# Window attention with two feed-forward stages on one core: the first four attention units multiply float32 as it is, and ScalarE issues four of the first loads

## The chip, the cores and the metric

One NeuronCore of a Trainium2 chip runs the whole program in one launch. The metric is the device time of one execution in microseconds (us). Engines are called as in the profile: PE (TensorE, with PEld for its weight loads), ACT (ScalarE), DVE (VectorE), POOL (GpSimd), SP (SyncE, which here only issues DMAs).

## What is computed

Three parts follow each other. q and k come as the reference draws them; only shapes matter here.

```python
# attention: B=2, H=8, S=576, D=64; window 128, causal, linear bias per head
scores = scale * q @ k.T ; masked to 0 <= i-j < 128, plus bias
attn   = softmax(scores) ; out = attn @ v             # float32
x      = out, heads joined: 1152 tokens x 512
# four experts, all of them for every token: h = relu(x @ w1[e]); y += p[:, e] * (h @ w2[e])
# last: h = relu(y @ w_in); out = (h * h) @ w_out      # w_in 512x2048, w_out 2048x512
```

Float32 accuracy is asked for. The kernel gets it by splitting each operand into a rounded part (float32r, "hi") and the rest ("lo") and adding up the products of the parts that matter.

## The kernel before, in words

**Attention** is cut into 20 units. The first four (numbers 0 to 3, one pair of heads each, `t0 == 0`) hold the first 128 queries of both batches: four score blocks of 128x128 each. The other sixteen hold two query tiles of one batch, with a window of two key tiles. For each unit the tasks are, in the names of the code: `load_q`, `load_k`, `load_v` (SP issues them, into the tiles `rq`, `rk`, `rv`); `qh`, `ql` (hi and lo of q), `kh`, `kl` (hi and lo of k, stacked in the 128 partitions of `khl`), `vh`, `vl` (hi and lo of v, written into two padded tiles); then per query tile `scores` (tile `sc`, two matmuls per head: `khl` with `qh`, `khl` with `ql`), `top` (DVE adds the bias and takes the extreme), `exp` (ACT), `inv` (DVE), `norm` (POOL), `turn` (PE transposes into `tp`), `hi` and `lo` (tile `pt`, both parts of the weights); and at the end `pv` (tile `xps`: per pair of heads and block three products, hi-hi, hi-lo, lo-hi, for each head), `evh`, `evl` (into `xh`, `xl`).

**The expert weights** are loaded as float32 (`wraw`) and split into `wh`, `wl` by ACT, DVE and POOL. The first expert's matmuls (`hps` for the first product, `yacc` for the second) run between the attention units as soon as their tokens are there.

**The order** of all this is set by a list planner (`Plan`): each task has prices per engine, dependencies, buffers that it takes (`SLOTS` gives the number of each) and a due time. At each step it takes the engine that can start first, and on it the task that is due first. A PE task that starts before `COLD` is priced 1.7 times as long. What it emits is a fixed order on each engine, in which every instruction waits for semaphores. Transfers use eight semaphores in turn (`DMAHW0` to `DMAHW7`), and a transfer is issued only when the one before it on the same semaphore has landed. After the planned part, from the second expert on, the order is a plain loop: four experts and two halves of the last stage, PE all the time.

The names that the change touches: `Plan.COLD`, `SLOTS["rv"]`, `VS` (blocks per `rv` tile), `unit_tasks` with `load_q`, `load_k`, `load_v` and `pv`, `job_tasks` with `scores` and `hi`, the due times at the calls, and `T0`.

Of the kernel before, what the change touches and what calls it, by code (L numbers as in the profile page):

```python
# [8 lines left out]
F32 = mybir.dt.float32  # L9
F32R = mybir.dt.float32r  # L10
# [6 lines left out]
P = 128  # L17
# [17 lines left out]
class Plan:  # L35
# [4 lines left out]

    LOOK = 0.15
    OTHER = 0.3
    COLD = 28.0

    def __init__(self, slots):
        self.tasks = []
# [80 lines left out]
def kernel(  # L127
# [14 lines left out]
    nc = tc.nc  # L142
    B, H, _, S = qT.shape
# [170 lines left out]
    def chunks(e):  # L314
# [1 line left out]


    SLOTS = dict(
        rq=3, rk=3, rv=2, qh=2, ql=2, khl=2, vp=2, sc=2, tp=2, ts=5, st=5, pt=2, work=2, y=2, h=4
    )  # L320
    plan = Plan(SLOTS)
    actx = ExitStack()
# [13 lines left out]
    def a_tile(kind, shape, dtype):  # L336
        return asp.tile(shape, dtype, tag=kind, name=kind, bufs=SLOTS[kind])
# [12 lines left out]
    def act(n, lat=0.1):  # L350
        return ("ACT", 0.1 + 0.00083 * n, 0.1 + 0.00083 * n + lat)

    def dve(n, lat=0.05):
        return ("DVE", 0.15 + 0.00105 * n, 0.15 + 0.00105 * n + lat)

    def gps(n, lat=0.05):
        return ("POOL", 0.2 + 0.0021 * n, 0.2 + 0.0021 * n + lat)

    def pe(us):
        return ("PE", us, us + 0.25)  # L360
# [28 lines left out]
                    out=bias[:, h, cs], in0=rel[:, cs], scalar1=scale, scalar2=None, op0=ALU.mult  # L389
                )  # L390

    VS = 4
    vpad = []
    for i in range(2):
        vh = abias.tile([P, VS, 3, D], F32R, name=f"vh{i}")
# [15 lines left out]
    def unit_tasks(u, due):  # L411
# [30 lines left out]

        def load_v(eng):
            t = b_["rv"].tile = a_tile("rv", [P, VS, 2 * D], F32)
            cs = slice(c * 2 * D, (c + 1) * 2 * D)
            for i, b in enumerate(bs):
                nc.sync.dma_start(
                    out=t[:, i * full:(i + 1) * full, :],
                    in_=v[b, k0:k0 + full * P, cs].rearrange("(k p) d -> p k d", p=P),
                )  # L450
                if left:
                    nc.sync.dma_start(out=t[0:left, full, :], in_=v[b, k0 + full * P:q1, cs])

        def dma(kb, n):
            return [("SP", max(0.5 * n, kb / 210.0), max(0.5 * n, kb / 210.0) + 2.2)]
# [31 lines left out]
        def vl(eng):  # L487
            for r, k in parts:
# [2 lines left out]
        end = due[-1]  # L491
        first = due[0]
        kbytes = nb * 2 * D * 4 / 1024.0
        lq = add("lq", dma(2 * kbytes * nq, nb), load_q, takes=[b_["rq"]], due=first - 12.0,
                 follow=[task.get(("lq", u - 1))])
        lk = add("lk", dma(kbytes * nk, nb), load_k, takes=[b_["rk"]], due=first - 11.9,
                 follow=[task.get(("lk", u - 1))])
        lv = add("lv", dma(kbytes * nk, nb + bool(left)), load_v, takes=[b_["rv"]],
                 due=end - 9.0, follow=[task.get(("lv", u - 1))])
        tqh = add("qh", [act(G * nq), dve(G * nq)], qh, shared=True, deps=[lq], takes=[b_["qh"]],  # L500
                  bufs=[b_["rq"]], due=first - 9.0)
        tkh = add("kh", [act(G * nk), dve(G * nk)], kh, shared=True, deps=[lk], takes=[b_["khl"]],
                  bufs=[b_["rk"]], due=first - 9.1)
        tql = add("ql", [gps(G * nq), dve(G * nq)], ql, shared=True, deps=[tqh], takes=[b_["ql"]],
                  bufs=[b_["rq"], b_["qh"]], due=first - 8.2)
        tkl = add("kl", [dve(G * nk), gps(G * nk)], kl, shared=True, deps=[tkh],
                  bufs=[b_["rk"], b_["khl"]], due=first - 8.3)
        nv = nb * nk
        tvh = add("vh", [act(nv), dve(nv)], vh, shared=True, deps=[lv, task["zero", u % 2]], takes=[b_["vp"]],
                  bufs=[b_["rv"]], due=end - 3.4)  # L510
        tvl = add("vl", [gps(nv), dve(nv)], vl, shared=True, deps=[tvh], bufs=[b_["rv"], b_["vp"]],
                  due=end - 2.6)

        split = []
        wide = 0
# [1 line left out]
            wide += tile_n(t) * (1 if t == 0 else 2)  # L517
        pos = 0
        for i, t in enumerate(range(t0, t1)):
            split += job_tasks(u, i, t, add, b_, due[i], [tqh, tql, tkh, tkl], G, q0, k0, pos, wide)  # L520
            pos += tile_n(t) * (1 if t == 0 else 2)

        mm = []
# [35 lines left out]
        def evl(eng):  # L559
            rest(eng, xl[:, c, cols], b_["work"].tile, xh[:, c, cols])  # L560

        tpv = add("pv", [pe(sum(3 * (max(0.107, w * 0.00046) + max(0.06, w * 0.00046))
                                for *_, w in mm))], pv,
                  deps=split + [tvh, tvl], takes=[b_["work"]], bufs=[b_["pt"], b_["vp"]],
                  due=end - 1.3, follow=[prev["pv"]])
        teh = add("evh", [act(nb * nq), dve(nb * nq)], evh, deps=[tpv], bufs=[b_["work"]],
                  due=end - 0.9)
# [2 lines left out]
    def job_tasks(u, i, t, add, b_, end, ready, G, q0, k0, pos, wide):  # L570
# [16 lines left out]
        def scores(eng):  # L587
            sc = s["sc"].tile = ps_tile("sc", [P, G, w], "sc")
            qs = slice(t * P - q0, t * P - q0 + n)
            for g in range(G):  # L590
                for ql in (b_["qh"].tile, b_["ql"].tile):
# [54 lines left out]
            parts = [(r, k * n, n) for k, r in enumerate(rows)]  # L646

        def hi(eng):
            if i == 0:
# [16 lines left out]

        tb = [task["bias", c, True]] + ([task["bias", c, False]] if t else [])
        tsc = stage("sc", [pe(2 * G * max(0.107, w * 0.00047))], scores, 7.4, deps=ready,
                    takes=[s["sc"]], bufs=[b_["qh"], b_["ql"], b_["khl"]])
# [9 lines left out]
        m = G * len(cols) * n  # L679
        thi = stage("hi", [act(m), dve(m)], hi, 2.0, deps=[ttp],  # L680
                    takes=[b_["pt"]] if i == 0 else [], bufs=[s["tp"]] + ([b_["pt"]] if i else []))
        tlo = stage("lo", [dve(m)], lo, 1.5, deps=[thi], bufs=[s["tp"], b_["pt"]])
        return [thi, tlo]

# [400 lines left out]
```

## Time and profile before

| | |
|---|---|
| median of 3 runs | 706.04 us (705.80 to 706.08) |
| profiled execution | 706.03 us; its span, first to last instruction, 704.2 us |
| busy share of the span | PE 98%, PEld 88%, DVE 45%, ACT 38%, POOL 30% |
| chain that ended last | PE 89% of the span, nearly all of it `yacc` and `hps` |
| DMA | 48.12 MB, mean 68 GB/s |
| granted TensorE clock | 1.00 in every slice of the page |

Busy PE time counts a matmul from its start to its end, and matmuls overlap; how fast PE goes is read from the distance between the starts of two that follow each other (called the pitch below). Engines other than PE cost time only where PE waits for them.

### The profile page before, as it was taken

The page shows a single profiled execution, that of the slowest core. Times are in us where ns is not written, and L with a number is a line of the kernel's source. Part 1 is how long each engine was busy: PE and PEld are TensorE (multiplying, and loading weights), DVE is VectorE, ACT ScalarE, POOL GpSimd, SP SyncE. Part 2 cuts the span into 40 slices and gives each one's busy share as a digit, 9 for nine tenths or more (in the row PEclk, how much of TensorE's full clock was granted, in tenths as well). Part 3 has the DMA queues.
Part 4 walks back from the last instruction along what each step waited for, and adds up shares of the span by engine and source line. Part 5 has one row for each costly group of instructions (what it writes and reads, how often), then busy time and mean ns, then how long its engine had stood idle before and what let it go on. Part 6 is the DMA issues. An engine that isn't in the chain of part 4 may idle for free.

```text
span 704.2 us, 9937 instructions
## 1 busy us (share of the span) xinstructions
PE 686.7 (98%) x3796; PEld 622.1 (88%) x3796; DVE 314.0 (45%) x718; ACT 264.4 (38%) x606; POOL 211.8 (30%) x222
## 2 busy tenths in 40 slices
PE   4999999999999999999999999999999999999997
PEld 3889898889999999999999999999999999999996
DVE  6789888732121212121122655527786627112121
ACT  6898576624331112311112322314354434322221
POOL 5899756407550003510011000000232222222221
PEclk9999999999999999999999999999999999999999
DMA  5863321223410001310005500035400120001011
GB/s 144 236 205 98 92 75 46 70 95 116 125 56 0 1 28 62 120 31 0 1 31 177 182 2 0 31 108 197 144 1 1 31 90 1 1 0 46 1 45 46
DMA packets 39137, 48.12 MB, mean 68 GB/s; under 512 B 3633, under 2 KB 27697, under 8 KB 39089
## 3 DMA queue, kind: packets, MB, share of 16 engines
q1 hardware_dynamic: 39088, 47.48, 21.6%
q8 instruction: 30, 0.49, 0.3%
q14 instruction: 19, 0.15, 0.1%
HBM read 45.11 MB, written 2.36 MB: 67 GB/s over the span
## 4 chain that ended last, share of the span: by engine, by line
PE 89%; DVE 0%; issue 0%
PE yacc L740 41%; PE hps L706 41%; PE xps L547 3%; PE tp L638 1%; PE sc L592 1%; PE xtp L772 1%; DVE y L764 0%
## 5 line engine op out<-in xcount | busy, mean ns | idle before, releaser
L706 PE MATMUL hps<-xh,wh 128*128 128x384 f32 (+1 forms) x608 | 201.9, 332 | 0.8 <-DVE xl L347 0.5
L706 PE MATMUL hps<-xl,wh 128*128 128x384 f32 (+1 forms) x608 | 199.8, 329 | 1.1 <-DVE xl L347 1.1
L706 PE MATMUL hps<-xh,wl 128*128 128x384 f32 (+1 forms) x608 | 200.2, 329 | 0.0
L740 PE MATMUL yacc<-wh,hl 128*128 128x512 f32 x432 | 170.9, 396 | 0.0
L740 PE MATMUL yacc<-wl,hh 128*128 128x512 f32 x432 | 170.6, 395 | 0.0
L740 PE MATMUL yacc<-wh,hh 128*128 128x512 f32 x432 | 168.9, 391 | 0.0
L722 DVE SCALAR_TENSOR_TENSOR hl<-hps,hh 128x384 fp32r<-128x384 f32 x80 | 44.6, 558 | 227.6 <-ACT hh L721 227.6
L721 ACT ACTIVATE hh<-hps 128x384 fp32r<-128x384 f32 x80 | 39.3, 491 | 245.1 <-PE hps L706 245.1
L730 POOL TENSOR_TENSOR hl<-r,hh 128x384 fp32r<-128x384 f32 x48 | 50.8, 1059 | 265.9 <-ACT hh L729 265.9
L706 PEld LDWEIGHTS hps<-xh,wh 128*128 128x128 f32 x608 | 114.9, 189 | 7.0 <-issue 0.7
L706 PEld LDWEIGHTS hps<-xl,wh 128*128 128x128 f32 x608 | 114.8, 189 | 6.6 <-DVE xl L347 1.4
L706 PEld LDWEIGHTS hps<-xh,wl 128*128 128x128 f32 x608 | 114.7, 189 | 0.0
L273 POOL TENSOR_TENSOR wl<-wraw,wh 128x1024 fp32r<-128x1024 f32 x24 | 57.2, 2390 | 175.3 <-ACT wh L271 167.9
L740 PEld LDWEIGHTS yacc<-wh,hl 128*128 128x128 f32 x432 | 81.1, 188 | 17.4
L740 PEld LDWEIGHTS yacc<-wl,hh 128*128 128x128 f32 x432 | 81.1, 188 | 13.2
L740 PEld LDWEIGHTS yacc<-wh,hh 128*128 128x128 f32 x432 | 81.3, 188 | 12.6
L728 DVE TENSOR_TENSOR r<-hps,r 128x384 f32<-128x384 f32 x48 | 26.7, 556 | 102.6 <-ACT r L727 102.6
L727 ACT ACTIVATE r<-hps 128x384 f32<-128x384 f32 x48 | 23.6, 491 | 92.0 <-PE hps L706 92.0
L628 POOL TENSOR_SCALAR ts<-ts,st 128x256 f32<-128x256 f32 (+2 forms) x80 | 40.0, 514 | 22.9 <-DVE st L623 18.1
L613 ACT ACTIVATE ts<-ts,st 128x256 f32<-128x256 f32 (+2 forms) x80 | 37.1, 466 | 5.0 <-DVE st L604 5.0
L729 ACT ACTIVATE hh<-r 128x384 fp32r<-128x384 f32 x48 | 25.2, 526 | 35.6 <-DVE r L728 35.6
L547 PE MATMUL xps<-pt,vh 128*128 128x128 f32 (+3 forms) x224 | 34.9, 261 | 0.0
(71 smaller groups left out, 715.3 us busy)
## 6 DMA issues: line engine op xcount, KB each, us to landing
wraw<-in_w_dram SPq DMA_DIRECT2D x32, 512.0 KB, 4.1
wraw<-in_w_in_dram SPq DMA_DIRECT2D x16, 512.0 KB, 4.1
wraw<-in_w_out_dram SPq DMA_DIRECT2D x16, 512.0 KB, 4.5
rq<-in_qT_dram SPq DMA_DIRECT2D x8, 256.0 KB, 4.2
out_dram<-y SPq DMA_DIRECT2D x8, 256.0 KB, 2.1
rk<-in_kT_dram SPq DMA_DIRECT2D x8, 192.0 KB, 5.0
rv<-in_v_dram SPq DMA_DIRECT2D x8, 192.0 KB, 2.6
rq<-in_qT_dram SPq DMA_DIRECT2D x8, 192.0 KB, 2.4
```

What stands on the lines that cost most here:

```text
L273: eng.tensor_tensor(out=lo[:, ks, :], in0=full, in1=f32(hi[:, ks, :]), op=ALU.subtract)
L547: nc.tensor.matmul(out=xps[0:rows, o0:o0 + w], lhsT=l_, rhs=r_, start=start, stop=(i == len(mm) - 1 and a == 0 and l_ is wl_), skip_group_ ...
L613: nc.scalar.activation(out=ts[0:n, g, :], in_=ts[0:n, g, :], func=ACTF.Exp, bias=st[0:n, 0, g:g + 1], scale=-1.0, accum_out=st[0:n, 1, g:g ...
L628: nc.gpsimd.tensor_scalar(out=ts[0:n, g, :], in0=ts[0:n, g, :], scalar1=st[0:n, 2, g:g + 1], scalar2=1.0, op0=ALU.mult, op1=ALU.mult,)
L706: nc.tensor.matmul(out=ps, lhsT=l_[:, k, cs], rhs=r_[:, k, cols], start=(k == 0 and r_ is xh and l_ is wh and not second), stop=(k == KT - ...
L721: nc.scalar.activation(out=hh, in_=ps, func=ACTF.Relu)
L722: nc.vector.scalar_tensor_tensor(out=hl, in0=ps, scalar=0.0, in1=f32(hh), op0=ALU.max, op1=ALU.subtract)
L727: nc.scalar.activation(out=r, in_=ps, func=ACTF.Relu)
L728: nc.vector.tensor_tensor(out=r, in0=ps, in1=r, op=ALU.mult)
L729: nc.scalar.activation(out=hh, in_=r, func=ACTF.Copy)
L730: nc.gpsimd.tensor_tensor(out=hl, in0=r, in1=f32(hh), op=ALU.subtract)
L740: nc.tensor.matmul(out=y, lhsT=l_[:, ns], rhs=r_[:, fo, :], start=(f == 0 and j == 0), stop=(f == FT - 1 and j == 2),)
```

## The change

The first four units (`raw`) no longer split q, k, v and the softmax weights: q is loaded once into 64 partitions, the score matmul takes `rk` and `rq` as float32, one per head; the transposed weights are copied to `pt` once; and `pv` takes `rv` and `pt` as float32, one matmul of 64 columns per head and batch. In units 0 and 1 the second batch's part of q and k is issued from ACT's queue. v of a raw unit is one transfer, `rv` tiles have three blocks and there are four of them. The planner gets other numbers: COLD, the due times of all units and of the first weights.

```diff
-    COLD = 28.0
+    COLD = 20.0
...
-        rq=3, rk=3, rv=2, qh=2, ...
+        rq=3, rk=3, rv=4, qh=2, ...
...
-    VS = 4
+    VS = 3
...
+        raw = t0 == 0
...
         def load_q(eng):
+            r = D if raw else P
             t = b_["rq"].tile = a_tile("rq", [P, G, nq], F32)
             for i, b in enumerate(bs):
-                nc.sync.dma_start(
-                    out=t[:, 2 * i:2 * i + 2, :],
-                    in_=qT[b, 2 * c:2 * c + 2, :, q0:q1].rearrange("a p s -> p a s"),
+                (nc.scalar if i and u < 2 else nc.sync).dma_start(
+                    out=t[0:r, 2 * i:2 * i + 2, :],
+                    in_=qT[b, 2 * c:2 * c + 2, 0:r, q0:q1].rearrange("a p s -> p a s"),
                 )
         def load_k(eng):
...
-                nc.sync.dma_start(
+                (nc.scalar if i and u < 2 else nc.sync).dma_start(
...
         def load_v(eng):
...
+            if raw:
                 nc.sync.dma_start(
+                    out=t[:, 0:nb, :], in_=v[:, 0:P, cs].rearrange("b p d -> p b d")
+                )
+                return
...
-        tqh = add("qh", ...)
+        if not raw:
+            tqh = add("qh", ...)
...
         def pv(eng):
             xps = b_["work"].tile = ps_tile("work", [P, nb * nq], "xps")
+            if raw:
+                for i in range(nb):
+                    for a in range(2):
+                        nc.tensor.matmul(
+                            out=xps[a * D:(a + 1) * D, i * P:(i + 1) * P],
+                            lhsT=b_["rv"].tile[:, i, a * D:(a + 1) * D],
+                            rhs=b_["pt"].tile[:, 2 * i + a, :], start=True, stop=True,
+                            skip_group_check=True,
+                        )
+                return
...
             for g in range(G):
+                if raw:
+                    nc.tensor.matmul(
+                        out=sc[0:n, g, :], lhsT=b_["rq"].tile[0:D, g, qs],
+                        rhs=b_["rk"].tile[:, g, j0:j0 + w], start=True, stop=True,
+                    )
+                    continue
...
+        if raw:
+            return [thi]
         tlo = stage("lo", [dve(m)], lo, 1.5, deps=[thi], bufs=[s["tp"], b_["pt"]])
...
-            unit_tasks(u, [20.0 + 2.0 * u])
+            unit_tasks(u, [14.0 + 2.0 * u])
...
-            end = 45.0 + 5.5 * (u - NP)
+            end = 38.0 + 5.5 * (u - NP)
...
-    T0, T1, ITEM = 34.0, 34.0, 4.2
+    T0, T1, ITEM = 24.0, 34.0, 4.2
```

Three places where the order moves. **ACT, from its first instruction**; `rq`, `rk` are the raw loads, `bias` the table of biases, `ts` the scores in softmax, and what an instruction waits for stands in brackets (DMAHW0 to 7 are the transfers' semaphores). Before:

```order
L384 ACT_TABLE_LOAD
L384 ACTIVATE bias<-rel 128x128 [waits Pool_49]
L384 ACTIVATE bias<-rel 128x128 x5
L341 ACTIVATE qh<-rq 128x512 [waits DMAHW1_49,DMAHW0_49]
L341 ACTIVATE khl<-rk 64x512 [waits DMAHW3_49,DMAHW2_49]
```

And now:

```order
L434 DMA rq<-in_qT_dram 64x2x128
L442 DMA rk<-in_kT_dram 64x2x128
L434 DMA rq<-in_qT_dram 64x2x128
L384 ACT_TABLE_LOAD
L384 ACTIVATE bias<-rel 128x128 [waits Pool_49]
L384 ACTIVATE bias<-rel 128x128
L442 DMA rk<-in_kT_dram 64x2x128 [waits DMAHW5_49]
L384 ACTIVATE bias<-rel 128x128 x4
L643 ACTIVATE ts,st<-ts,st 128x128 [waits DVE_49] x12
```

The splits of q and k are gone from the front, four transfers have come in, and the fourth of them, the second batch's k of unit 1, waits for the fifth of the transfers' semaphores, ahead of four biases and all exponentials.

**SP, from its first instruction**, as it is now:

```order
L434 DMA rq<-in_qT_dram 64x2x128
L442 DMA rk<-in_kT_dram 64x2x128
L434 DMA rq<-in_qT_dram 64x2x128
L442 DMA rk<-in_kT_dram 64x2x128
L451 DMA rv<-in_v_dram 128x2x128
L434 DMA rq<-in_qT_dram 64x2x128 [waits DMAHW0_49]
L434 DMA rq<-in_qT_dram 64x2x128 [waits DMAHW1_49]
L442 DMA rk<-in_kT_dram 64x2x128 [waits DMAHW2_49]
L442 DMA rk<-in_kT_dram 64x2x128 [waits DMAHW3_49]
L451 DMA rv<-in_v_dram 128x2x128 [waits DMAHW4_49]
L434 DMA rq<-in_qT_dram 64x2x128 [waits DMAHW5_49,PE_49]
```

Before, SP's first four rows were two q and two k transfers of unit 0 alone. The third and the eleventh row here are the first and second transfer on semaphore DMAHW5; the eleventh is unit 3's first q, which also waits for the scores of unit 0 on PE. ACT's fourth transfer waits for a count of 32 on that semaphore, which is both of them landed.

**PE, at the end of the last 128-wide scores.** Before, a piece of 48 matmuls for `xps` in the four units begins like this:

```order
L592 MATMUL sc<-khl,ql 128x128
L547 MATMUL xps<-pt,vh_97 128x128 x2
L547 MATMUL xps<-pt,vl_98 128x128
L547 MATMUL xps<-pt,vh_97 64x128 x2
L547 MATMUL xps<-pt,vl_98 64x128
```

And now PE's whole beginning is:

```order
L616 MATMUL sc<-rk,rq 128x128 x16
L668 MATMUL tp<-ident,ts 128x128 x8
L554 MATMUL xps<-pt,rv 64x128 x8
L668 MATMUL tp<-ident,ts 128x128 x8
L745 MATMUL hps<-xh,wh 128x256
L745 MATMUL hps<-xl,wh 128x256
L745 MATMUL hps<-xh,wl 128x256
L554 MATMUL xps<-pt,rv 64x128 x8
```

32 score matmuls of the four units have become 16, 48 for `xps` have become 16, and all four units' scores now stand ahead of the first transposes.

## Rows read from the trace of the kernel before

**Rows 1.** Busy time by stretch (stretch, length, engines (xinstructions), granted clock, DMA share, GB/s).

```profile
0.00:10.00 10.00, 3.21 (x14) 3.02 (x15) 5.79 (x22) 5.75 (x13) 4.05 (x14) 1.00 0.49 126
0.00:20.00 20.00, 10.09 (x42) 8.76 (x43) 12.69 (x55) 12.92 (x41) 11.76 (x26) 1.00 0.63 159
20.00:50.00 30.00, 27.89 (x201) 25.70 (x200) 24.95 (x69) 26.86 (x73) 27.57 (x33) 1.00 0.81 233
50.00:80.00 30.00, 28.35 (x219) 26.04 (x218) 26.68 (x74) 23.42 (x64) 28.28 (x32) 1.00 0.33 91
80.00:120.00 40.00, 40.00 (x324) 36.85 (x323) 34.13 (x111) 28.14 (x89) 23.78 (x40) 1.00 0.25 67
```

**Rows 2.** PE's waits, whole span: for whom, total us, times, longest.

```profile
PE sc L592 <- DVE khl L347: 6.8, 2, 6.4
PE sc L592 <- POOL khl L347: 3.1, 2, 2.3
```

**Rows 3.** Timeline, PE from 17.3 to 30.7 (start us, us, engine, line, operation).

```profile
17.32 0.47 PE L592 MATMUL sc<-khl,qh 128*128 128x128 f32 x1 [0.87 <-POOL khl L347]
17.59 0.41 PE L592 MATMUL sc<-khl,ql 128*128 128x128 f32 x1
17.80 0.42 PE L592 MATMUL sc<-khl,qh 128*128 128x128 f32 x1
...
25.49 1.08 PE L638 MATMUL tp<-ident,ts 128*128 128x128 f32 x4
...
26.79 0.41 PE L592 MATMUL sc<-khl,qh 128*128 128x256 f32 x1
27.00 0.41 PE L592 MATMUL sc<-khl,ql 128*128 128x256 f32 x1
...
28.44 0.28 PE L592 MATMUL sc<-khl,qh 128*128 128x256 f32 x1
28.55 0.28 PE L592 MATMUL sc<-khl,ql 128*128 128x256 f32 x1
...
30.68 0.33 PE L706 MATMUL hps<-xh,wh 128*128 128x256 f32 x1
```

**Rows 4.** Timeline, all engines, the first 8 us; SPq is SP issuing.

```profile
0.73 0.96 SPq L430 DMA_DIRECT2D rq<-in_qT_dram  x2
...
4.34 1.26 SPq L438 DMA_DIRECT2D rk<-in_kT_dram  x2
...
5.64 1.07 SPq L447 DMA_DIRECT2D rv<-in_v_dram  x2
...
6.44 0.48 PE L592 MATMUL sc<-khl,qh 128*128 128x128 f32 x1 [6.44 <-DVE khl L347]
...
7.36 0.63 ACT L341 ACTIVATE khl<-rk 64x512 fp32r<-64x512 f32 x1 [0.50 <-DMA rk<-in_kT_dram]
```

**Rows 5.** Groups by line and shape, ACT to 160 us: busy us, mean ns.

```profile
L341 ACT ACTIVATE qh<-rq 128x512 fp32r<-128x512 f32 x12 | 7.5, 626 | 4.4 <-DMA rq<-in_qT_dram 3.3 <-DVE st L604 1.1
...
L613 ACT ACTIVATE ts<-ts,st 128x128 f32<-128x128 f32 x16 | 6.2, 388 | 0.0
...
L341 ACT ACTIVATE vh<-rv 128x256 fp32r<-128x256 f32 x10 | 4.1, 410 | 0.5 <-DMA rv<-in_v_dram 0.5
...
L384 ACT ACTIVATE bias<-rel 128x128 bf16<-128x128 f32 x6 | 1.3, 296 | 0.1
L384 ACT ACT_TABLE_LOAD x1 | 1.3, 1283 | 0.7 <-PEq L1075 0.7
```

**Rows 6.** Timeline, POOL from 13 to 19.

```profile
13.01 0.73 POOL L347 TENSOR_TENSOR vl<-rv,vh 128x256 fp32r<-128x256 f32 x1
13.72 2.20 POOL L628 TENSOR_SCALAR ts<-ts,st 128x128 f32<-128x128 f32 x4
16.01 1.26 POOL L347 TENSOR_TENSOR khl<-rk,khl 64x512 fp32r<-64x512 f32 x1
17.36 1.41 POOL L628 TENSOR_SCALAR ts<-ts,st 128x128 f32<-128x128 f32 x4
```

More of the change, by code (lines that the diff above doesn't have):

```diff
@@ L318 @@
     SLOTS = dict(
-        rq=3, rk=3, rv=2, qh=2, ql=2, khl=2, vp=2, sc=2, tp=2, ts=5, st=5, pt=2, work=2, y=2, h=4
+        rq=3, rk=3, rv=4, qh=2, ql=2, khl=2, vp=2, sc=2, tp=2, ts=5, st=5, pt=2, work=2, y=2, h=4
     )
@@ L445, in load_v @@
             cs = slice(c * 2 * D, (c + 1) * 2 * D)
-            for i, b in enumerate(bs):
+            if raw:
                 nc.sync.dma_start(
-                    out=t[:, i * full:(i + 1) * full, :],
-                    in_=v[b, k0:k0 + full * P, cs].rearrange("(k p) d -> p k d", p=P),
-                )
-                if left:
-                    nc.sync.dma_start(out=t[0:left, full, :], in_=v[b, k0 + full * P:q1, cs])
+                    out=t[:, 0:nb, :], in_=v[:, 0:P, cs].rearrange("b p d -> p b d")
+                )
+                return
+            b = bs[0]
+            nc.sync.dma_start(
+                out=t[:, 0:full, :],
+                in_=v[b, k0:k0 + full * P, cs].rearrange("(k p) d -> p k d", p=P),
+            )
+            if left:
+                nc.sync.dma_start(out=t[0:left, full, :], in_=v[b, k0 + full * P:q1, cs])
         def dma(kb, n):
@@ L493, in unit_tasks @@
         kbytes = nb * 2 * D * 4 / 1024.0
-        lq = add("lq", dma(2 * kbytes * nq, nb), load_q, takes=[b_["rq"]], due=first - 12.0,
+        lq = add("lq", dma((1 if raw else 2) * kbytes * nq, 1 if u < 2 else nb), load_q, takes=[b_["rq"]], due=first - 12.0,
                  follow=[task.get(("lq", u - 1))])
-        lk = add("lk", dma(kbytes * nk, nb), load_k, takes=[b_["rk"]], due=first - 11.9,
+        lk = add("lk", dma(kbytes * nk, 1 if u < 2 else nb), load_k, takes=[b_["rk"]], due=first - 11.9,
@@ L497, in unit_tasks @@
                  follow=[task.get(("lk", u - 1))])
-        lv = add("lv", dma(kbytes * nk, nb + bool(left)), load_v, takes=[b_["rv"]],
+        lv = add("lv", dma(kbytes * nk, 1 + bool(left)), load_v, takes=[b_["rv"]],
                  due=end - 9.0, follow=[task.get(("lv", u - 1))])
[L500 to L512, printed above, removed]
+        if not raw:
+            tqh = add("qh", [act(G * nq), dve(G * nq)], qh, shared=True, deps=[lq], takes=[b_["qh"]],
+                      bufs=[b_["rq"]], due=first - 9.0)
+            tkh = add("kh", [act(G * nk), dve(G * nk)], kh, shared=True, deps=[lk], takes=[b_["khl"]],
+                      bufs=[b_["rk"]], due=first - 9.1)
+            tql = add("ql", [gps(G * nq), dve(G * nq)], ql, shared=True, deps=[tqh], takes=[b_["ql"]],
+                      bufs=[b_["rq"], b_["qh"]], due=first - 8.2)
+            tkl = add("kl", [dve(G * nk), gps(G * nk)], kl, shared=True, deps=[tkh],
+                      bufs=[b_["rk"], b_["khl"]], due=first - 8.3)
+            nv = nb * nk
+            tvh = add("vh", [act(nv), dve(nv)], vh, shared=True, deps=[lv, task["zero", u % 2]], takes=[b_["vp"]],
+                      bufs=[b_["rv"]], due=end - 3.4)
+            tvl = add("vl", [gps(nv), dve(nv)], vl, shared=True, deps=[tvh], bufs=[b_["rv"], b_["vp"]],
+                      due=end - 2.6)
@@ L519, in unit_tasks @@
         for i, t in enumerate(range(t0, t1)):
-            split += job_tasks(u, i, t, add, b_, due[i], [tqh, tql, tkh, tkl], G, q0, k0, pos, wide)
+            split += job_tasks(
+                u, i, t, add, b_, due[i], [lq, lk] if raw else [tqh, tql, tkh, tkl], G, q0, k0,
+                pos, wide,
+            )
             pos += tile_n(t) * (1 if t == 0 else 2)
@@ L560, in evl @@
             rest(eng, xl[:, c, cols], b_["work"].tile, xh[:, c, cols])
-        tpv = add("pv", [pe(sum(3 * (max(0.107, w * 0.00046) + max(0.06, w * 0.00046))
-                                for *_, w in mm))], pv,
-                  deps=split + [tvh, tvl], takes=[b_["work"]], bufs=[b_["pt"], b_["vp"]],
+        us = sum(3 * (max(0.107, w * 0.00046) + max(0.06, w * 0.00046)) for *_, w in mm)
+        tpv = add("pv", [pe(1.0 if raw else us)], pv, deps=split + ([lv] if raw else [tvh, tvl]),
+                  takes=[b_["work"]], bufs=[b_["pt"], b_["rv" if raw else "vp"]],
                   due=end - 1.3, follow=[prev["pv"]])
@@ L575, in job_tasks @@
         w = (0 if t == 0 else P) + n
+        raw = t == 0
         s = {k: Buf(k) for k in ("sc", "ts", "st", "tp")}
@@ L590, in scores @@
             for g in range(G):
+                if raw:
+                    nc.tensor.matmul(
+                        out=sc[0:n, g, :], lhsT=b_["rq"].tile[0:D, g, qs],
+                        rhs=b_["rk"].tile[:, g, j0:j0 + w], start=True, stop=True,
+                    )
+                    continue
                 for ql in (b_["qh"].tile, b_["ql"].tile):
@@ L648, in hi @@
         def hi(eng):
+            if raw:
+                t_ = b_["pt"].tile = a_tile("pt", [P, 2, 8 * P], F32R).rearrange(
+                    "p s w -> p (s w)"
+                )[:, 0:G * n].bitcast(F32).rearrange("p (g w) -> p g w", g=G)
+                rounded(eng, t_, s["tp"].tile)
+                return
             if i == 0:
@@ L668, in job_tasks @@
         tsc = stage("sc", [pe(2 * G * max(0.107, w * 0.00047))], scores, 7.4, deps=ready,
-                    takes=[s["sc"]], bufs=[b_["qh"], b_["ql"], b_["khl"]])
+                    takes=[s["sc"]],
+                    bufs=[b_[k] for k in (("rq", "rk") if raw else ("qh", "ql", "khl"))])
         tmx = stage("mx", [("DVE", G * (0.16 + 0.001 * w), G * (0.16 + 0.001 * w) + 0.1)], top, 6.4,
@@ L681, in job_tasks @@
                     takes=[b_["pt"]] if i == 0 else [], bufs=[s["tp"]] + ([b_["pt"]] if i else []))
+        if raw:
+            return [thi]
         tlo = stage("lo", [dve(m)], lo, 1.5, deps=[thi], bufs=[s["tp"], b_["pt"]])
```

## The prediction

> **What bounds the kernel now.** I begin with busy time by stretch [rows 1]; its engine columns are PE, PEld, DVE, ACT and POOL. From 80 us on PE is busy 40.00 of 40 us, and from there to the end the order is a plain loop on PE. What the change can move is therefore where PE stands when the helpers no longer hold it: idle time of PE, or slow work of PE, ahead of 80 us. PE is idle 9.91 us of the first 20, then 2.11 up to 50 and 1.65 up to 80: 13.7 us in all, nearly three quarters of it at the start. In the stretches from 20 to 80 us the helpers are close to full too: POOL has 27.57 and 28.28 of 30 us, ACT 26.86 and 23.42, DVE 24.95 and 26.68.
>
> The waits of PE say what the start waits for [rows 2]: 6.4 us for the first `khl`, and 3.1 us more for `khl` that POOL finishes. PE's own rows give a second cost [rows 3]. A 256-column product stands 0.21 us from the next at 26.79 and 27.00, and 0.11 at 28.44 and 28.55: that is 256 columns at 1.2 and at 2.4 GHz. The granted-clock column reads 1.00 all along, so the pitch is what tells it here. Ahead of about 28.3 us PE work costs double; the last long wait of PE ended at 17.32.
>
> The profiled execution, 706.03 us, is the median within 0.01. Its span is 704.2, and I leave the 1.8 us around it as it is.
>
> **The change, part by part.** *First matmul.* Before, one queue issues two q and two k transfers, and then ACT and DVE split them [rows 4]: the second k is issued half way through the pair at 4.34 (1.26 us for two, 0.63 each, so at 4.97) and ACT is let go at 7.36, 2.39 after. Now each queue issues one q and one k. SP's second starts at 0.73 + 0.63 = 1.36 and lands 2.39 later, at about 3.8, and no split stands behind it. For an issue by ACT there is no row; the nearest are SP's pairs, 0.96 to 1.26 us for two, and I take 0.63. First matmul 3.8 against 6.44: 2.6 earlier.
>
> *The price of a float32 matmul.* No row has one. From below: the float32r product of the same 128x128 shape, pitch 0.21 [rows 3]; a float32 transpose of that shape is 1.08 / 4 = 0.27. From above: four float32r products, 0.86, if each of two parts of both operands makes a full one. I take 0.43: in the scores one float32 matmul of 64 rows takes the place of two float32r products, which hold the same four combinations of parts, two of them stacked in 128 rows. The Trainium skill, "FP8 and Floating Point Precision", section on TensorE precision, says that true float32 takes four passes through the array; with 128 columns at the low clock that is an estimate of 0.43 a matmul, no row here shows it, and by it the sum below stays as it is. At 0.43 PE gains nothing by itself while the clock is low: scores 16 x 0.43 = 6.9 against 32 x 0.21 = 6.9, and `xps` 16 x 0.43 = 6.9 against at most 48 x 0.21 = 10.1 (its 64-row products may take less). What there is beyond that has to come from what PE waits for.
>
> *The new wait.* Unit 0's four matmuls end at 3.8 + 4 x 0.43 = 5.5. SP's third and fourth transfers, unit 1's first half, start by 2.62 and land at 5.0, so two more matmuls end at 6.4. Then PE needs unit 1's second k. ACT issues it only when SP's eleventh transfer has landed. SP comes to that at 0.73 + 8 x 0.63 + 2 x 0.535 (`rv`, 1.07 for two [rows 4]) = 6.84; unit 0's scores are done then, so it lands at about 9.25. ACT issues from 9.25 to 9.9 and the k lands at 11.65. PE stands from 6.4 to 11.65, 5.25 us. So early idle is 3.8 + 5.25 = 9.05 against 9.91 in the first 20 us: the 2.6 us of the first matmul are nearly all given back.
>
> *What is queued behind it.* On ACT stand four biases and all exponentials. It goes on at 9.9; four biases at 0.22 end at 10.8, and unit 0's exponentials, 4 x 0.388 [rows 5], at 12.3. DVE's inverse now stands behind unit 1's tops, whose scores end at 11.65 + 2 x 0.43 = 12.5; with 1.3 us for two tops and the inverse (an estimate without a row, 0 at the least) POOL begins unit 0's norm at 13.8. Before it did at 13.72 [rows 6]: POOL gains nothing at its first norm, though the splits are gone.
>
> *PE to the end of the first four units.* Ten more scores: 11.65 + 4.3 = 15.95. The transposes of units 0 and 1 need two norms, 13.8 + 2.20 + 1.41 = 17.4 [rows 6], and end at 17.9; a copy to `pt` of 128x512, as long as a `qh` of that shape, 0.63 [rows 5], then eight `xps` at 0.43 to 21.9; eight transposes at 0.27 to 24.1; three products of `hps` at 0.21; eight `xps` to 28.2, all at the low clock. If the clock rises as much earlier as PE's last long wait ends earlier (11.65 against 17.32), it does so at 22.65 instead of 28.3, and the same work ends at about 25.5. Before, this point lies at 30.68 [rows 3], but PE had by then also done work that now comes later: three more `hps` at 0.21 and four wide scores at 0.21 at the low clock, four at 0.11: about 2.0. So 28.7 is to be compared. PE leads by 0.5 (low clock) to 3.2 us (early rise).
>
> *What of that lead lasts.* Up to 80 us the helpers are nearly full, so PE's lead is kept only as far as they are ahead. ACT had been busy 5.75 us of its first 10 [rows 1]; now, until 9.9, it does the table load and two biases, 1.28 + 0.44 = 1.72, so 4.0 less. Taken from it are four `qh` and two of the `khl` at 0.63 and four `vh` at 0.41 [rows 5], 5.4. ACT leads by 1.4. POOL starts its norms level (13.8 against 13.72), and behind that point one `khl`, 1.26, and one `vl`, 0.73, are gone [rows 6]: it leads by 1.9. DVE loses its share of the splits and four `lo` and is the least full to 50 us. POOL, the fullest, sets the pace; its 1.9 lies inside PE's 0.5 to 3.2. I take **-1.9 us**.
>
> The rest costs nothing that I can see: v of a raw unit is one transfer for two (SP issues only, and `rv` is used last), the zeroing of the padded v tiles is shorter, where POOL waits afterwards anyway, and the due times move the same work forward on a PE that is full from 80 us on. If POOL's cover at the start goes, nothing else waits there.
>
> Sum: 706.03 - 1.9 = 704.1.
>
> **Rivals.** *A, PE's whole lead counts.* If the early rise of the clock is real and the helpers, relieved of the first splits, keep up, or if a float32 matmul costs 0.21, the 3.2 stay: 702.8. For it: some 2.1 us of PE idle from 20 to 50 are there to be won. Against: POOL's 27.57 of 30.
>
> *B, the lead is eaten later.* The list of tasks is ordered by prices that know nothing of the wait on ACT, so exponentials, splits of weights and norms stand in an order made for a start 5 us earlier; PE then idles between 25 and 50 us where it idled at the start: 706.0. For it: three helpers over 80% busy, which leave little to catch up with.
>
> *C, slower: a float32 matmul costs 0.86.* Scores then end at 11.65 + 8.6 = 20.25, transposes 22.4, copy 23.0; with the clock up, eight `xps` 3.44, transposes 1.08, `hps` 0.32, `xps` 3.44: 31.3 against 28.7, on PE itself, with no cover: +2.6, 708.6. It decides from about 0.65 a matmul on, where the same chain reaches 28.7.
>
> *D, the change does more than I think: the wait doesn't bind.* If SP's eleventh transfer lands before ACT comes to the wait (the issues would have to take about 0.3 us instead of 0.48 to 0.63), PE goes on at once, idle falls by up to 5.25 and at most 3.5 more than my forecast are won after PE's later waits: 700.6. The row for SP's issues speaks against it.
>
> **How the numbers follow.** A measurement of this kernel can tell about 0.2%, 1.4 us, from no change. Forecast 0.42: its size is POOL's 1.9 and may fall to ACT's 1.4 or rise a little, so it lies over the 1.4 a little more often than not. A 0.20, B 0.18, C 0.14, D 0.06. Faster: 0.27 of the forecast, A and D whole, 0.53. Slower: 0.13 of C and 0.04 of B, where the order costs more than it gains, 0.17. Within 0.2%: 0.30. The range goes from 701.0, below A by the 1.8 us that the estimated terms may give (1.3 for the inverse, 0.5 for shorter issues), to C's 708.6; left out are D and the part of C in which the clock stays low.
>
> **What would show it.** Right: the first `sc` at about 3.8; among PE's waits one of about 5.2 us for a `rk` transfer, ending near 11.7; ACT idle some 5 us ahead of its fourth transfer; float32 matmuls 0.43 apart; the pitch of PE halved near 23 us; POOL's first norm near 13.8; in the table by stretch about 0.9 us less idle in the first 20 us and PE full from 80 us on. Wrong: a pitch of 0.21 or 0.86, a fourth transfer of ACT that goes out early, or, with the start as forecast, PE idle growing in 20 to 50 us by as much as it fell before.

## The result: slower, and the profile after

The changed kernel took 710.81 us (median of 4 runs, 708.92 to 711.13); the kernel before, in the same session, 705.93 (705.80 to 706.08). The ratio is 1.0064, 95% interval 1.0048 to 1.0080: slower by some 4.9 us, where 1.9 less was forecast, and above the range's upper end. The profiled execution is at the top, 711.13 us, its span 709.3, 5.1 more than before.

Busy time by stretch of the changed kernel, with the columns of [rows 1]:

```profile
0.00:20.00 20.00, 8.99 (x40) 8.53 (x40) 6.50 (x48) 7.89 (x32) 5.96 (x21) 1.00 0.57 145
20.00:50.00 30.00, 23.14 (x139) 19.02 (x138) 23.87 (x55) 21.15 (x59) 24.85 (x28) 0.83 0.83 222
50.00:80.00 30.00, 29.64 (x235) 27.41 (x234) 27.04 (x66) 24.33 (x63) 27.04 (x30) 1.00 0.31 85
80.00:120.00 40.00, 39.26 (x307) 35.91 (x308) 31.72 (x106) 26.59 (x82) 24.22 (x37) 1.00 0.30 82
```

PE's idle time is 20 less its first column: 11.0 us in the first stretch (9.9 before), 6.9 in the second (2.1), 0.4 and 0.7 after that (1.65 and none). In sum 5.3 us more than before, about the size of the loss; 4.75 of it lie between 20 and 50 us. The granted clock is no longer 1.00 there but 0.83. And no helper is full in that stretch: ACT has 21.15 of 30, before 26.86. Every engine waits for part of it.

PE's waits over the whole span (for whom, total us, times, longest), against [rows 2]:

```profile
PE sc L616 <- DMA rk<-in_kT_dram: 11.0, 2, 6.6
PE hps L745 <- DVE xl L347: 2.8, 1, 2.8
PE sc L622 <- DVE khl L347: 2.0, 1, 2.0
PE tp L668 <- POOL ts L658: 1.5, 3, 1.1
```

And PE's timeline, against [rows 3] (start us, us, engine, line, operation, count, idle before):

```profile
4.45 2.90 PE L616 MATMUL sc<-rk,rq 64*128 64x128 f32 x12 [4.45 <-DMA rk<-in_kT_dram]
13.91 4.60 PE L616 MATMUL sc<-rk,rq 64*128 64x128 f32 x20 [6.57 <-DMA rk<-in_kT_dram]
18.44 1.97 PE L668 MATMUL tp<-ident,ts 128*128 128x128 f32 x8
20.34 1.98 PE L554 MATMUL xps<-pt,rv 128*64 128x128 f32 x16
...
25.08 1.14 PE L554 MATMUL xps<-pt,rv 128*64 128x128 f32 x16
26.15 0.39 PE L745 MATMUL hps<-xh,wh 128*128 128x256 f32 x1
...
30.05 0.58 PE L745 MATMUL hps<-xl,wh 128*128 128x256 f32 x1 [2.80 <-DVE xl L347]
...
30.86 0.41 PE L622 MATMUL sc<-khl,ql 128*128 128x256 f32 x1
31.07 0.41 PE L622 MATMUL sc<-khl,qh 128*128 128x256 f32 x1
...
33.09 0.28 PE L745 MATMUL hps<-xh,wl 128*128 128x256 f32 x1
33.20 0.28 PE L745 MATMUL hps<-xh,wh 128*128 128x256 f32 x1
...
40.97 0.89 PE L668 MATMUL tp<-ident,ts 128*128 128x128 f32 x4 [1.14 <-POOL ts L658]
43.83 0.55 PE L622 MATMUL sc<-khl,qh 128*128 128x256 f32 x1 [1.97 <-DVE khl L347]
...
44.82 0.63 PE L779 MATMUL yacc<-wh,hh 128*128 128x512 f32 x1
45.25 0.63 PE L779 MATMUL yacc<-wl,hh 128*128 128x512 f32 x1
...
51.08 0.28 PE L745 MATMUL hps<-xh,wh 128*128 128x256 f32 x1
51.19 0.28 PE L745 MATMUL hps<-xl,wh 128*128 128x256 f32 x1
```

Three things stand here. First, the wait for unit 1's second k, 6.57 us up to 13.91. Second, by 26.15 the four units are done all the same, where the kernel before had the same work done at 28.7 by the prediction's count: PE was 2.5 us *ahead*. Third, the lead is lost behind that. PE stands 2.80 us for `xl`, later 1.14 and 1.97, and after the first and the last of these places the pitch of 256 columns is 0.21 again instead of 0.11 (0.43 for 512). The granted clock of these stretches says the same:

```profile
29.50:32.90 3.40, 2.85 (x13) 2.85 (x14) 3.40 (x5) 0.00 (x0) 3.17 (x2) 0.50 1.12 287
43.20:49.90 6.70, 6.07 (x24) 5.52 (x25) 5.34 (x11) 3.70 (x9) 6.37 (x7) 0.50 0.49 137
```

PE works at the low clock from 30.05 to 32.9 and from 43.8 to 50.0, 9.0 us. From 26.15 on the bill is 3.9 us of idle time more than before, plus half of 9.0, less the 1.1 us that the kernel before lost to its own low clock up to 28.3: 7.3. From 2.5 ahead to 5.1 behind is 7.6, so the bill is nearly complete.

What ACT and SP did at the start, and what DVE, POOL and ACT did around the 2.80 us:

```profile
1.54 0.82 SPq L442 DMA_DIRECT2D rk<-in_kT_dram  x1
...
7.69 1.25 SPq L434 DMA_DIRECT2D rq<-in_qT_dram  x2
...
10.34 0.60 ACTq L442 DMA_DIRECT2D rk<-in_kT_dram  x1
10.99 0.91 ACT L384 ACTIVATE bias<-rel 128x128 bf16<-128x128 f32 x4 [6.40 <-DMA rq<-in_qT_dram]
11.80 0.39 ACT L643 ACTIVATE ts<-ts,st 128x128 f32<-128x128 f32 x1
...
16.66 2.99 POOL L658 TENSOR_SCALAR ts<-ts,st 128x128 f32<-128x128 f32 x8 [12.70 <-DVE st L653]
...
22.27 0.69 DVE L347 TENSOR_TENSOR wl<-wraw,wh 128x512 fp32r<-128x512 f32 x1
...
25.46 1.99 POOL L347 TENSOR_TENSOR ql<-rq,qh 128x512 fp32r<-128x512 f32 x1
26.34 3.32 DVE L347 TENSOR_TENSOR wl<-wraw,wh 128x512 fp32r<-128x512 f32 x2
27.41 1.70 POOL L347 TENSOR_TENSOR wl<-wraw,wh 128x512 fp32r<-128x512 f32 x1
29.59 0.41 DVE L347 TENSOR_TENSOR xl<-xps,xh 128x256 fp32r<-128x256 f32 x1
...
34.12 0.39 ACT L1020 ACTIVATE hh<-hps 128x256 fp32r<-128x256 f32 x1 [5.27 <-PE hps L745]
```

ACT stood 6.40 us in front of its fourth transfer, as forecast (the row names `rq`, which SP's eleventh transfer loads), and everything behind it came late: unit 0's exponentials at 11.80, POOL's first norm at 16.66 (13.72 before, [rows 6]). Around 27 us the chain reads backwards: ACT waits 5.27 us for PE's first finished `hps`; PE waits for `xl`; `xl` stands on DVE behind two splits of weights that take 3.32 us. From 29.5 to 32.9 ACT does nothing at all.

### The profile page after: what moved, and what is told of

It reads as the page before. It is cut to its first block, busy times and chain, and to the rows that moved or that the text cites. A ratio compares the mean times of both kernels' runs of the same rounds, so it can differ in the third digit from the quotient of the medians.

```text
span 709.3 us, 9847 instructions
## 1 busy us (share of the span) xinstructions
PE 686.7 (97%) x3780; PEld 620.3 (87%) x3780; DVE 308.1 (43%) x704; ACT 259.6 (37%) x598; POOL 208.2 (29%) x216
## 4 chain that ended last, share of the span: by engine, by line
PE 93%; DMA 2%; ACT 2%; SPq 1%; DVE 1%; issue 0%; POOL 0%; POOLq 0%; DVEq 0%; ACTq 0%
PE yacc L779 42%; PE hps L745 42%; PE xps L570 4%; PE tp L668 2%; PE sc L622 2%; DMA wraw<-in_w_dram 1%; DMA rq<-in_qT_dram 1%; PE sc L616 1%; PE xtp L811 1%; ACT wh L341 1%; DMA rk<-in_kT_dram 0%; ACT ts L643 0%; DVE khl L347 0%; SPq L442 0%; SPq L434 0%
## 5 line engine op out<-in xcount | busy, mean ns | idle before, releaser
L634 DVE CUSTOM_DVE_ANT_0 ts<-sc,bias 128x256 f32<-128x256 f32 (+2 forms) x80 | 26.9, 377 | 14.9 <-PE sc L616 11.1
```

The costliest lines, as they stand in the source:

```text
L634: nc.vector.tensor_tensor_reduce(out=s["ts"].tile[0:n, g, :], in0=s["sc"].tile[0:n, g, :], in1=bias[0:n, 2 * c + g % 2, off:off + w], scal ...
```

## The experiments

Two theories. **W**: the wait on ACT's queue is the loss, and all that follows is its echo. **O**: the planner's new numbers make an order that loses after the first units, wherever these end. A third, **C** (not the prediction's rival C), concerns the price of the clock's falls. Each run was set against the kernel before on the same chip (medians 705.9 to 706.4).

### The wait taken away, two ways

One transfer is moved to SP; PE, DVE and POOL keep every instruction in its place.

```diff
 def load_k(eng):
-                (nc.scalar if i and u < 2 else nc.sync).dma_start(
+                (nc.scalar if i and u < 1 else nc.sync).dma_start(
```

> Changed kernel, but the second batch's k of unit 1 is issued by SP behind the first; the order on PE, DVE and POOL stays the same to the row, ACT loses only that transfer. Theory W (the wait on ACT is the loss): PE's 6.6 us wait before unit 1's second half falls under 1 us, all that follows comes some 5 us earlier, and the time falls by 4.5 to 6 us, to 705 to 706.5. Rival O (the order after the first units is the loss: transfers of weights and DVE's place for xl and khl set the gaps near 27 and 40 us): the front gets 5 us shorter, but PE waits as much longer at 25 to 45 us, and the time falls by under 1.5 us, to 709.3 or more. In between, both.

706.31 us (10 runs, 705.28 to 708.27), 4.5 less than the changed kernel and level with before (ratio 1.0004, 0.9994 to 1.0013). W's number came out. But PE's timeline shows what O foresaw too:

```profile
9.00 2.04 PE L616 MATMUL sc<-rk,rq 64*128 64x128 f32 x8 [0.35 <-DMA rk<-in_kT_dram]
12.44 2.04 PE L616 MATMUL sc<-rk,rq 64*128 64x128 f32 x8 [1.40 <-DMA rk<-in_kT_dram]
...
26.03 0.39 PE L745 MATMUL hps<-xl,wh 128*128 128x256 f32 x1 [2.81 <-DVE xl L347]
...
37.07 0.90 PE L668 MATMUL tp<-ident,ts 128*128 128x128 f32 x4 [1.13 <-POOL ts L658]
39.93 0.36 PE L622 MATMUL sc<-khl,qh 128*128 128x256 f32 x1 [1.97 <-DVE khl L347]
```

The 6.57 us have become 0.35 and 1.40 for two later transfers, and the later gaps are the same to 0.01 us, only 4 us earlier. They are not made by the wait; they belong to the order.

The second way leaves the transfer on ACT, but directly behind ACT's third one, ahead of the activation table:

```diff
 def load_q(eng):
...
+            if u == 1:
+                load_k(eng, (1,))
```

> Changed kernel, new numbers; the second k of unit 1 stays in ACT's queue but stands directly behind ACT's third transfer, ahead of the activation table and the biases, so that it no longer waits for SP's eleventh transfer; SP, PE, DVE and POOL keep their order. If the wait for a shared transfer semaphore is the cause, and not ScalarE's queue as such: PE's 6.6 us wait falls under 1.5 us and the time is that of the run with this k on SP, 706.3, or up to 1 us less (SP issues one transfer fewer). If issuing from ScalarE itself costs: 708.5 to 711.

705.98 us (ratio to before 0.9995, 0.9985 to 1.0004), with a second wait of 1.44 us instead of 6.57. So it is the turn on a shared transfer semaphore, for which ACT waited until SP's eleventh transfer had landed, and not issuing from ScalarE as such.

### All transfers back on SP

```diff
-                (nc.scalar if i and u < 2 else nc.sync).dma_start(
+                nc.sync.dma_start(
```

> Changed kernel with all q and k transfers issued by SP, as before; PE, DVE and POOL keep their order to the row. This takes back the ScalarE queue part of the change alone. Theory W: no wait of 6.6 us either; unit 0's second batch lands about 1.3 us later than in the run with only k of unit 1 moved, so the time is that run's plus 0 to 1.3, 705 to 707.5. Rival O: 709 to 711 like the changed kernel, because the front does not decide.

708.21 us (1.0028, 1.0017 to 1.0040): 1.9 more than with three transfers on ACT, where 0 to 1.3 were expected; a miss, between the ranges of W and O. Without the wait, the ScalarE queue is worth 1.9 us here.

### The planner's numbers

```diff
-    COLD = 20.0
+    COLD = 28.0
...
-            unit_tasks(u, [14.0 + 2.0 * u])
+            unit_tasks(u, [20.0 + 2.0 * u])
...
-            end = 38.0 + 5.5 * (u - NP)
+            end = 45.0 + 5.5 * (u - NP)
...
-    T0, T1, ITEM = 24.0, 34.0, 4.2
+    T0, T1, ITEM = 34.0, 34.0, 4.2
```

> Changed kernel with the planner's numbers of before (COLD 28, first units due from 20, later ones from 45, weights from 34); raw units and the ACT queue as changed, so the wait of about 6.6 us on ACT stays. Theory W: the same as the changed kernel within 1.5 us, 709.5 to 712. Rival O (the new numbers crowd transfers of weights and q, k, v into 20 to 37 us, where the 16 DMA engines are full, and put xl and khl late on DVE): the long gaps of PE at 27 and 44 us shrink to under 1.5 us each, the clock falls once at most, 706.5 to 708.5.

704.82 us (0.9976, 0.9967 to 0.9986), though ACT's wait is still there: 6.0 less than the changed kernel, more than O had asked for, and faster than before. Two views of this run, PE's wait for unit 1's second k and the stretch from 20 to 50 us:

```profile
12.89 4.60 PE L616 MATMUL sc<-rk,rq 64*128 64x128 f32 x20 [4.88 <-DMA rk<-in_kT_dram]
...
20.00:50.00 30.00, 25.70 (x195) 21.98 (x192) 25.36 (x68) 27.16 (x77) 25.07 (x29) 1.00 0.88 241
```

PE is busier by 2.6 us there than in the changed kernel, ACT by 6.0, and the clock stays at 1.00. A part of the 6.0 us lies ahead of that stretch: the wait is 4.88 us instead of 6.57 (PE also began 0.7 later) and ends 1.0 earlier, at 12.89, since this k landed 2.6 us after its issue instead of 3.4. In the 20 to 37 us that O named, the share of the DMA engines falls from 1.09 to 0.97, as O would have it. But it is 1.11 in the run with k on SP and 1.11 and 1.12 in the two repaired versions below, which are 4.5 and 4.7 us faster, so the crowding of transfers that O named is not the mechanism.

The same four edits the other way round, put into the kernel before without any float32 unit:

```diff
-    COLD = 28.0
+    COLD = 20.0
...
-    T0, T1, ITEM = 34.0, 34.0, 4.2
+    T0, T1, ITEM = 24.0, 34.0, 4.2
```

> Kernel before with the new planner's numbers alone (COLD 20, due times 14, 38, 24); splits and SP queue as before. Theory W: no new wait at the front, 705.5 to 707. Rival O: the same numbers make the same gaps between 20 and 50 us, at least one fall of the clock, 707.5 to 710.

706.24 us (0.9997, 0.9988 to 1.0007): nothing. The new numbers lose only together with the float32 units; O's form of them, a bad table in itself, is out.

Both repairs together (the one line of k on SP and the four numbers of before), and then the early issue from ACT (its two lines) with those numbers:

```diff
-                (nc.scalar if i and u < 2 else nc.sync).dma_start(
+                (nc.scalar if i and u < 1 else nc.sync).dma_start(
...
-    T0, T1, ITEM = 24.0, 34.0, 4.2
+    T0, T1, ITEM = 34.0, 34.0, 4.2
```

> Changed kernel with the planner's numbers of before and with k of unit 1 issued by SP: both repairs together. If the wait on ACT (worth 4.5 us in the run with the new numbers) and the crowded order (worth 6.0 us with the wait in place) are two causes that add, the time is 710.8 - 4.5 - 6.0 = 700.3, between 699.5 and 701.5, and PE has no gap over 1.2 us between 20 and 50 us. Rival: the old numbers fit only because the start is late, and the early start runs into POOL and DVE at 25 to 40 us: 702.5 to 704.5.

> The same early issue from ACT, with the planner's numbers of before: the version without either of the two costs found. With the run with k on SP and old numbers at 701.8: 700.5 to 701.8, since SP's transfers come one issue of 0.6 us earlier. Rival: the third semaphore turn on ACT delays the biases and exponentials, 702 to 703.5.

701.77 us (0.9938, 0.9926 to 0.9950) and 701.58 (0.9931, 0.9919 to 0.9944). The two costs nearly add, 9.0 us of 10.5; the first version lies just above the range for a clean sum. Both versions beat both kernels, the second by 4.5 us of before's 706.12. What the numbers give with k on SP shows in the first 80 us, first with the new numbers, then with those of before:

```profile
0.00:80.00 80.00, 65.00 (x443) 57.73 (x444) 62.09 (x185) 56.31 (x161) 60.03 (x80) 0.96 0.59 159
0.00:80.00 80.00, 69.12 (x481) 61.21 (x482) 59.80 (x198) 62.99 (x181) 59.84 (x85) 0.98 0.63 164
```

PE is idle 15.0 us with the new numbers and 10.9 with the old, 4.1 less, and its clock is down again for 6.8 us and for 3.4. So waiting is the larger part of what the numbers cost, and the clock the smaller. PE's longest wait behind 20 us is now 1.1 us.

### The parts alone

Float32 units with all transfers on SP and the numbers of before (the first edit, on the changed kernel); and the ScalarE queue put into the kernel before, splits and numbers kept (the second, in both loads):

```diff
-                (nc.scalar if i and u < 2 else nc.sync).dma_start(
+                nc.sync.dma_start(
...
-    T0, T1, ITEM = 24.0, 34.0, 4.2
+    T0, T1, ITEM = 34.0, 34.0, 4.2
```

```diff
-                nc.sync.dma_start(
+                (nc.scalar if i and u < 2 else nc.sync).dma_start(
```

> Float32 units alone: all transfers on SP and the planner's numbers of before. From the run with k of unit 1 on SP and old numbers (701.8) the ScalarE queue is taken away, which cost 1.9 us with the new numbers (708.2 against 706.3): 703 to 704.5. Rival, the later second batch is hidden: 701.8 to 702.5. If float32 as such did not pay: 706 or more.

> Kernel before with the ScalarE queue part alone (second batch's q and k of units 0 and 1 issued by ACT; splits and numbers of before). ACT's third and fourth transfers stand behind biases there and wait for transfers of SP too, so the first khl comes some 2 us earlier and the second unit's later: 705 to 707.5. If the queue alone were a gain: 703.5 to 704.9.

703.53 us (0.9963, 0.9949 to 0.9977) and 707.73 (1.0023, 1.0014 to 1.0032). The float32 units are worth 2.6 us. The queue alone *loses* 1.6, a little beyond what was expected: there ACT's third and fourth transfers both wait behind biases for transfers of SP, and PE gets its first `khl` at 9.45 instead of 6.44. All medians in one table:

| units and transfers | numbers of before | new numbers |
|---|---|---|
| split, all on SP | 706.0 to 706.4 (before) | 706.24 |
| split, four on ACT | 707.73 | not run |
| float32, all on SP | 703.53 | 708.21 |
| float32, four on ACT, the last one waiting | 704.82 | 710.81 (the change) |
| float32, three on ACT, one k on SP | 701.77 | 706.31 |
| float32, four on ACT, all early | 701.58 | 705.98 |

Down a column the wait costs 3.1 to 3.2 us (numbers of before) or 4.5 to 4.8 (there it is also the longer one, 6.57 against 4.88 us); across, the numbers cost 4.4 to 6.0 with float32 units and nothing with splits.

### What the new numbers lose

All from the run with k on SP and new numbers, 706.31. First, the two weight splits moved behind the `xl` of units 2 and 3 on DVE, nothing else (`lo` of the second block of weights is held back until `evl` of unit 3 has been emitted):

```diff
         def lo(eng, h):
+            if i == 1 and "evl3" not in held_lo:
+                held_lo[h] = eng
+                return
...
             rest(eng, xl[:, c, cols], b_["work"].tile, xh[:, c, cols])
+            if u == 3:
+                held_lo["evl3"] = True
+                for h in range(2):
+                    held_lo["fn"](held_lo[h], h)
```

> Kernel with k of unit 1 on SP and the new numbers (706.3), with one thing moved: two splits of weights (wl, 3.3 us together on DVE) stand behind the xl of units 2 and 3 instead of ahead of them. Theory O: PE's wait of 2.8 us for xl falls under 0.6 us and the clock does not fall near 28 us; the waits of 1.1 and 2.0 us at 37 and 40 us grow in part, because DVE still has the same work: 703 to 705. Rival (helpers are the bound, the place of a gap does not matter): all of the 2.8 us comes back at 30 to 42 us: 705.8 to 707.

705.90 us (0.9992, 0.9983 to 1.0001), within 0.4 of its base. The 2.81 us wait is gone, but three weight splits in a row then took DVE 5.3 us, PE waited 1.25, 0.95 and 1.23 elsewhere, the clock fell all the same (granted 0.5 from 22.8 to 26.2), and the gaps of 1.14 and 1.97 stayed. Taking away this one gap, alone, gains nothing clear of noise.

Second, the gaps filled with 50 extra products whose results are not used (24, 9 and 17 at the three places), so that PE has work there:

```diff
+    def filler(out, count):
+        for _ in range(count):
+            nc.tensor.matmul(
+                out=out, lhsT=w1t[0, 0][0][0][:, 0, 0:P], rhs=xh[:, 0, 0:2 * P], start=True,
+                stop=True, skip_group_check=True,
+            )
```

> Kernel with k of unit 1 on SP and the new numbers (706.3), with 24, 9 and 17 extra 256-column products on PE (results not used) in its three long gaps near 23, 36 and 38 us, at 0.117 us each; other engines keep their order. It prices the clock alone: low-clock stretches of 27.8 to 30.7 and 41.0 to 44.5 us run at half speed, 3.2 us lost at most. Theory C (the falls of the clock cost time): no low clock after 21 us, 703 to 705. Rival (the helpers would have held PE anyway): low clock gone, PE waits longer for POOL and DVE, 705.8 to 707.

704.72 us (0.9979, 0.9969 to 0.9988). No low clock behind 17.9 us, and 1.6 us gained, half of the 3.2 that were lost to it at most. Where the other half went, waits of PE elsewhere presumably, was not followed up.

Third, the same two weight splits moved further, behind unit 4's tops and the second `hl`:

```diff
         def lo(eng, h):
+            if i == 1 and "go" not in held_lo:
+                held_lo[h] = eng
+                return
...
+            if it == 1:
+                held_lo["go"] = True
+                for h in range(2):
+                    held_lo["fn"](held_lo[h], h)
```

> Kernel with k of unit 1 on SP and the new numbers (706.3); the two weight splits that stood ahead of xl on DVE (3.3 us) now stand behind the tops of unit 4 and the second hl; all else keeps its order. If DVE between 22 and 33 us holds up PE, ACT and POOL: PE's 2.8 us wait gone, ACT's wait for the first hh under 2 us, unit 4's tops some 4 us earlier, 702.5 to 704.5. If the order as a whole (PE takes the first expert's products early and then has nothing to do at 36 to 40 us) is the cause: the waits of 1.1 and 2.0 us there stay or grow, 705 to 706.5.

704.25 us (0.9971, 0.9961 to 0.9982), 2.1 less than its base, near the upper end of the first expectation. DVE's load between 22 and 28 us is therefore a part of it. Not all; the two later waits of PE came some 2.7 us earlier but stayed, as the second expectation had it of them:

```profile
34.51 0.89 PE L669 MATMUL tp<-ident,ts 128*128 128x128 f32 x4 [1.86 <-POOL ts L659]
37.10 0.55 PE L623 MATMUL sc<-khl,qh 128*128 128x256 f32 x1 [1.70 <-DVE khl L347]
```

Last, single numbers set back, the weights' due times in one run (first edit) and the units' in another (second):

```diff
-    T0, T1, ITEM = 24.0, 34.0, 4.2
+    T0, T1, ITEM = 34.0, 34.0, 4.2
```

```diff
-            unit_tasks(u, [14.0 + 2.0 * u])
+            unit_tasks(u, [20.0 + 2.0 * u])
...
-            end = 38.0 + 5.5 * (u - NP)
+            end = 45.0 + 5.5 * (u - NP)
```

> Kernel with k of unit 1 on SP and the new numbers (706.3), except that the weights' due times begin at 34 again instead of 24. If the early weights crowd DVE, POOL and the DMA engines, this alone gives most of what the old numbers gave: 701 to 703. If the units' due times or COLD matter more, 705 to 707.

> Kernel with k of unit 1 on SP (706.3) with only the units' due times set back (20 and 45 instead of 14 and 38); COLD 20 and weights from 24 as changed. If the units' due times make the 4.5 us between 706.3 and 701.8: 701.5 to 703. If it takes the balance of units and weights, which both sets of numbers had (weights 11 and 14 us ahead of the wide units) and this one has not: 705 to 708.

706.88 us (1.0005, 0.9996 to 1.0014) and 703.60 (0.9959, 0.9946 to 0.9971). Weights alone: nothing, a miss for that idea. Units alone: 2.7 of the 4.5 us. This lies between the two expectations. Which tasks changed places by it, and how COLD and T0 share the other 1.8 us, was not separated and stays open. ACT's busy time in 20 to 50 us doesn't tell these runs apart: with the weights' numbers set back it was 27.11 us, as in the fast versions, with the units' 22.34.

## Why the prediction was wrong

*What bounds the kernel*: right. The loss lies in PE's idle time and clock ahead of 80 us, and nothing behind 120 us changed.

*First matmul*: 4.45 for 3.8. The term was mis-sized by the issues, 0.75 and 0.82 us instead of 0.63, and by a landing 2.91 us after the issue instead of 2.39.

*The price of a float32 matmul*: right in the scores, 0.43 (each has two records, whose starts stand 0.213 us apart; with what stands around them 10 take 4.60 us). In `xps` 0.24 at the low clock (8 in 1.9) and 0.13 at the high one (8 in 1.07): half of the term, which gave PE 1.5 us on the first eight and 0.65 on the second. The prediction's rival C is out. The halving could have been read from the kernel before, where a product with 64 columns of weights (`128*64`) has a pitch of 0.11 at the low clock and one with 128 columns 0.21:

```profile
24.00 0.41 PE L547 MATMUL xps<-pt,vl 128*128 128x128 f32 x1
24.21 0.42 PE L547 MATMUL xps<-pt,vh 128*64 128x128 f32 x2
24.43 0.31 PE L547 MATMUL xps<-pt,vl 128*64 128x128 f32 x1
```

For the scores of before the prediction sums 32 x 0.21 to 6.9; it is 6.7, and nothing hangs on it.

*The new wait*: right in place and cause, 6.57 us instead of 5.25. SP's eleventh transfer began at 7.69 (6.84 forecast), ACT's fourth at 10.34 (9.25), and it landed 3.4 us later where 2.4 was taken. That the wait eats the earlier start was right: the first 20 us have 1.1 us more idle time, where 0.9 less was forecast.

*What is queued behind it*: right in kind; POOL's first norm stood at 16.66, not 13.8, so POOL lost 2.9 us at its start where it was said to begin level.

*PE to the end of the first four units*: 26.15, for 25.5 with the early rise of the clock. The pitch was halved at 22.7 (transposes at 22.70 and 22.81, granted clock 1.00 from 22.67), where 22.65 was forecast. That hit is luck: the forecast moved the rise with the end of the long wait, which came at 13.91 instead of 11.65, and by that reasoning the rise belonged at 24.9. The early clock and the cheaper `xps` paid for the longer wait. The lead of 2.5 us lies inside the 0.5 to 3.2.

*What of that lead lasts*: **this step failed**, with the sentence that the due times only "move the same work forward on a PE that is full from 80 us on". POOL's lead of 1.9 us was taken as the pace of the helpers, as if they worked without pause. They don't: in 20 to 50 us ACT's busy time fell from 26.86 to 21.15 us, with 5.27 us of waiting for PE in one piece. The order of each engine is fixed, and one late piece stops the others in a ring: PE for `xl`, `xl` behind weight splits on DVE, ACT behind PE's first `hps`. The ring is read from the waits; that it is what costs the time is shown in part only (0.4 us back without the wait for `xl`, 2.1 with DVE's splits moved further, 2.7 with the units' due times). Rival B named that place and that kind of loss, but priced it at no more than the lead; there was no term for the clock falling again, which the gaps brought twice. The runs show the size: 4.5 us for the numbers once the wait is gone, 6.0 with it. Had the numbers stayed as before, the change would have taken 704.82, near the 704.1 forecast, though that nearness proves nothing about the sum's single terms.

## What to carry to other kernels

A transfer that is issued from a computing engine's queue carries its wait into that queue: read in the built order which earlier transfer it waits for, and what stands behind it. Issued first of all, the ScalarE queue gained some 2 us here over SP alone; with one transfer behind two biases it cost 3 to 5 us more than that.

Numbers that steer a static order are a change of their own. Price them alone: run the new code with the old numbers before judging either (here 704.82 against 710.81, and the best of all with one transfer moved).

A saving is passed on only if every engine's fixed order lets it through. After a saving, read the idle time of the engine that bounds the kernel in the stretch behind it (PE here, 6.9 us in 20 to 50 against 2.1). A helper's busy time is no such sign: ACT's was 27.11 in a run of 706.88 us and 22.34 in one of 703.60.

## What the runs showed of the hardware

A float32 matmul of 128 moving columns took 0.43 us at the low clock with 128 columns of weights and 0.24 with 64, and the trace holds two records for each. The first is twice the pitch of the float32r product of the same 128x128 shape, 0.21 [rows 3]. The Trainium skill, "FP8 and Floating Point Precision", section on TensorE precision, states four passes for true float32; the 0.43 of the scores agrees with four passes of 128 columns at 1.2 GHz. The 0.24 of `xps` says nothing for or against it: its records start in pairs, 0.007 us apart (20.339 and 20.346, then 20.608 and 20.614), and no row shows whether a pair is one product or two heads.

DVE's split of 128x512 took 0.69 us at 22.27 and 1.66 in the pair at 26.34, while POOL ran splits of its own, which took 1.70 and 1.99 instead of the 1.28 of its `wl` at 24.21. No run separates the two engines, so that they slow each other is not shown.

The clock can fall some time after a gap: with k on SP, PE took up work at 26.03 after its 2.81 us wait and still ran at the high clock (pitch 0.12) until 27.2; the granted clock is 0.5 from there to 30.6, with a pitch of 0.21.
